# Spectral block: three real products per complex column, rows on row halves, later statistics in the MLP

## Chip, core and metric

One core of a Trainium2 chip runs the whole program. The metric is device microseconds, the median of three runs.

## What is computed

The reference is a two-branch block on x of 2048 x 512 in float32, with six modulation vectors (sa, ca, ga, sb, cb, gb) from a small product of c and w_mod:

```python
h = _layernorm(x) * (1 + ca) + sa
x = x + ga * irfft2(rfft2(h) * (w_r + 1j * w_i))     # over both axes, 2048 x 512
h = _layernorm(x) * (1 + cb) + sb
x = x + gb * (mish(h @ w1 + b1) @ w2)                # 512 -> 1376 -> 512
```

## The kernel before

The Fourier transforms are matrix products, in three stages, and the MLP follows as the fourth.

- Stage one (16 tiles of 128 rows): forward row and column products.
- Stage two (8 pairs of lane groups, with their complex weights): p2_in, p2_mul, p2_prod, p2_out. p2_out (line 531) leaves in PSUM what store_d copies to d, the input of stage three; d is held as two big tiles of eight row tiles each. In p2_out 16 matmuls contract over 64 partitions each, the two row halves in turn. store_d (lines 393 and 394) copies real and imaginary parts, and stores the real part once more with the sign turned as a third part, so that one slice of 128 columns serves as [re, im] and the next as [im, -re]. z_out and p2_out of the last pair end the stage; apply_gate (line 581) is one more product.
- Stage three (16 tiles): p3_col does a tile's inverse column products, eight matmuls of 128 x 128 for four column groups j, with kc (real and imaginary constants, 1 MB each) as moving operand; ScalarE copies the result to e; p3_row does four row products with kiv on tile n - 1, and VectorE adds the result to x. Beside them runs `prep`, a table by step that prepares the MLP: load_w1 and split_w1 (12 pieces of w1; each is cast to a high part on ScalarE, and GpSimd subtracts it for the low part), load_w2, sum_w2 (four differences on GpSimd into the one tile tsum), split_w2 (high and low part of a group of w2, group t = 1 to 5), norm_sums (statistics of a row tile, lines 127 and 128), norm_scale (Ln and Exp on ScalarE, lines 131 and 132, then five small operations on VectorE), keep (two normalised tiles), transpose_in and split_in (their transposes, high and low part h2).
- The MLP: 8 blocks of 256 rows, six items each (item i = 0 is the short one, 96 of the 1376 columns). mlp(s) is one item: up(s), the first products (line 805); front(s), Mish on ScalarE (813); halves(s - 1), casts on ScalarE (765) and subtractions on VectorE (766); back(s), sums on VectorE (827); down(s - 2), the second products of the item two back (855; 846 for the short item). At i = 3 norm_pair normalises the next block's two tiles (161), at i = 4 they are transposed (693) and split (701, 705, 706). At i = 1 and 2 of the next block the results are gathered and added to x.

Everything is in manual order: each engine's queue is the order in which the code issues. All DMAs go through SP's queue. Buffers come from rings of two: y, t, g1, g2, h in SBUF, and the PSUM banks A to D (two of each). The two loads of a w2 group take the two y buffers, so a group's load waits until the sums and splits of the group before are done.

Of the kernel before, what the change touches and what calls it, by code (L numbers as in the profile page):

```python
# [12 lines left out]
P = 128  # L13
# [18 lines left out]
def tile_spectral_block(ctx: ExitStack, tc: tile.TileContext, x_d, w1_d, b1_d, w2_d,  # L32
# [117 lines left out]
    def norm_scale(lo, hi):  # L150
        w = hi - lo
        pair = bank("C" if hi < N2 else "D")
        r, done = pair[:, 0:w], pair[:, 4:4 + w]
        norm_guess(lo, hi, r)
        norm_refine(lo, hi, 1, r, done)
        nc.vector.scalar_tensor_tensor(nmr[:, lo:hi], mv[:, lo:hi, 0], -1.0, done, op0=ALU.mult, op1=ALU.mult)
# [229 lines left out]
    dd = [big.tile([P, 8, 4, 3, NQ], F32, name=f"d{i}", tag=t) for i, t in enumerate(("da", "db"))]  # L386

    def store_d(ps, q0, nq, i, eng=None):
        src = ps[:, (4 - nq) * P:].rearrange("p (q a c) -> p a c q", q=nq, c=2)
        dst = dd[i].rearrange("p n d c q -> p (n d) c q")  # L390
        s = src[:, 32 * i:32 * i + 32]
        if eng is None:
            nc.scalar.copy(dst[:, :, 0:2, q0:q0 + nq], s)
            nc.scalar.mul(dst[:, :, 2, q0:q0 + nq], s[:, :, 0, :], -1.0)
# [177 lines left out]
    def mod_gate():  # L572
# [11 lines left out]
    kc = []  # L584
    wqb = pw.tile([P, 4, 2, 512], F32, name="wqb", tag="half")
    with tc.manual_schedule():
# [13 lines left out]
        for p in range(pairs):  # L600
# [50 lines left out]
    w2hi = pm.tile([P, 7, 256], F32R, name="w2hi")  # L651
# [56 lines left out]
    def p3_col(n):  # L708
        d = dd[n // 8][:, n % 8]
# [8 lines left out]
        st["e", n] = e  # L718

    def p3_row(n):  # L720
        e = st.pop(("e", n))
        px = bank("B")
        for j in range(4):
            nc.tensor.matmul(px[:, j * P:(j + 1) * P], e[:, j * P:(j + 1) * P], kiv[:, j, :],  # L724
                             start=True, stop=True)
        xn = x[:, n, :].rearrange("p (a b) -> p a b", b=4)
        nc.vector.tensor_tensor(xn, xn, px.rearrange("p (b a) -> p a b", b=4), op=ALU.add)

    def w2_space(t):
        if t == 2:  # L730
# [3 lines left out]
            w2[3] = [w2hi, v[:, 2]]  # L734
            w2["lo"] = w[:, 5376:5888]
        if t == 4:
# [4 lines left out]
            w2[0] = [w[:, 5376:5888], w2["lo"]]  # L741

# [21 lines left out]
    def split(h, l, r):  # L764
        nc.scalar.copy(h, r)  # L765
        nc.vector.tensor_tensor(l, r, plain(h), op=ALU.subtract)  # L766

    def split_w2(t, sums):
# [5 lines left out]
        if t == 3 and sums:  # L774
            nc.scalar.copy(h[:, 768:], tsum.rearrange("p e d -> p (e d)"))
        elif sums:
            split(h[:, 768:], l[:, 768:], tsum.rearrange("p e d -> p (e d)"))
# [382 lines left out]
```

## Time and profile before

| | us |
|---|---|
| median of three runs | 377.82 (377.52 to 378.47) |
| the profiled execution | 376.28 |
| its span, first to last instruction | 374.3 |
| stage three on PE, first column to last row | 90.6 to 135.7 |
| busy: PE, VectorE (DVE), ScalarE (ACT), GpSimd (POOL) | 368.0, 261.6, 213.9, 91.3 |

The granted TensorE clock was 0.998 throughout. PE is the matmul row, PEld its weight loads. A line of the chain or of a timeline has the start in us from the span's first instruction, the length, engine and line; in brackets stands how long the engine had been idle, and who released it. A profile counts each fp32 matmul as two records.

### The profile page before, as it was taken

The numbers are of one execution on the slowest core, as the hardware profiler recorded it, in microseconds if no ns is written. First come the engines' busy times: TensorE is split into PE (matmuls) and PEld (weight loads), VectorE is DVE, ScalarE is ACT, GpSimd is POOL, SyncE is SP. The second block draws the span as 40 slices with busy tenths as digits, with TensorE's granted clock in tenths as the row PEclk, the third lists the DMA queues.
The fourth block names the chain that finished last, engine by engine and source line by source line (L and its number), as shares of the span: only waits on it lengthen the run. The fifth ranks groups of instructions, "written<-read, shape, count | busy, mean of one in ns | idle before, by whom it ended". The sixth has DMA issues, their size and how long they took to land.

```text
span 374.3 us, 8202 instructions
## 1 busy us (share of the span) xinstructions
PE 368.0 (98%) x3245; PEld 349.6 (93%) x3245; DVE 261.6 (70%) x585; ACT 213.9 (57%) x487; POOL 91.3 (24%) x110
## 2 busy tenths in 40 slices
PE   8999999999999999999999999999999999999995
PEld 7899866658999999999999999999999999999995
DVE  2898989893878978767537646655754764776982
ACT  1788856855668447754634634654564563574540
POOL 0687725871884302300000000000000010017000
PEclk9999999999999999999999999999999999999999
DMA  7999998453332311000100100100100200212011
GB/s 253 380 321 350 341 383 310 146 199 132 105 89 70 101 30 57 2 2 0 59 2 0 58 3 0 58 2 0 58 1 2 80 0 2 81 56 90 2 56 56
DMA packets 20164, 36.81 MB, mean 98 GB/s; under 512 B 3712, under 2 KB 6624, under 8 KB 19872
## 3 DMA queue, kind: packets, MB, share of 16 engines
q1 hardware_dynamic: 20128, 36.31, 28.1%
q8 instruction: 25, 0.41, 0.4%
q14 instruction: 11, 0.09, 0.1%
HBM read 32.10 MB, written 4.20 MB: 97 GB/s over the span
## 4 chain that ended last, share of the span: by engine, by line
PE 94%; DVE 2%; DMA 1%; ACT 1%; issue 1%; SPq 0%; ACTq 0%
PE bank L805 32%; PE bank L855 24%; PE bank L531 4%; PE bank L504 4%; PE bank L715 4%; PE bank L714 4%; PE bank L724 4%; PE bank L211 3%; PE bank L256 3%; PE bank L846 3%; PE bank L871 2%; PE bank L693 2%; PE bank L479 1%; DMA wmc<-in_w_mod_dram 1%; PE bank L257 1%; PE bank L258 1%
## 5 line engine op out<-in xcount | busy, mean ns | idle before, releaser
L766 DVE TENSOR_TENSOR al<-buf,ah 128x512 fp32r<-128x512 f32 (+2 forms) x85 | 51.8, 629 | 63.1 <-ACT ah L765 62.9
L813 ACT ACTIVATE buf<-bank,b1n 128x256 f32<-128x256 f32 (+1 forms) x88 | 37.3, 471 | 90.8 <-PE bank L805 76.7
L805 PE MATMUL bank<-h2e,w1h 128*128 128x256 f32 (+1 forms) x352 | 62.3, 279 | 0.0
L805 PE MATMUL bank<-h2o,w1h 128*128 128x256 f32 (+1 forms) x352 | 62.1, 278 | 0.0
L805 PEld LDWEIGHTS bank<-h2e,w1h 128*128 128x128 f32 (+1 forms) x352 | 52.8, 185 | 0.0
L805 PEld LDWEIGHTS bank<-h2o,w1h 128*128 128x128 f32 (+1 forms) x352 | 52.8, 185 | 0.0
L805 PE MATMUL bank<-h2e,w1l 128*128 128x256 f32 (+1 forms) x176 | 48.8, 277 | 0.0
L805 PE MATMUL bank<-h2o,w1l 128*128 128x256 f32 (+1 forms) x176 | 48.8, 277 | 0.0
L785 POOL TENSOR_TENSOR buf<-buf,modr 128x512 f32<-128x512 f32 (+1 forms) x3 | 3.9, 1297 | 179.6 <-DMA buf<-in_B_w_dram 150.8
L765 ACT CAST ah<-buf 128x512 fp32r<-128x512 f32 (+2 forms) x85 | 43.3, 554 | 2.6 <-PE bank L871 1.6
L827 DVE TENSOR_TENSOR buf<-buf 128x128 f32<-128x128 f32 x148 | 42.5, 328 | 1.3
L855 PE MATMUL bank<-w2a,ah 128*128 128x256 f32 x161 | 33.3, 278 | 0.0
L805 PEld LDWEIGHTS bank<-h2e,w1l 128*128 128x128 f32 (+1 forms) x176 | 32.6, 185 | 0.0
L805 PEld LDWEIGHTS bank<-h2o,w1l 128*128 128x128 f32 (+1 forms) x176 | 32.6, 185 | 0.0
L855 PE MATMUL bank<-w2b,ah 128*128 128x256 f32 x147 | 30.6, 277 | 0.0
L855 PEld LDWEIGHTS bank<-w2a,ah 128*128 128x128 f32 x161 | 26.1, 188 | 0.0
L715 PE MATMUL bank<-kc,d 128*128 128x128 f32 x128 | 24.8, 275 | 0.0
L714 PE MATMUL bank<-kc,d 128*128 128x128 f32 x128 | 24.7, 275 | 0.0
L855 PEld LDWEIGHTS bank<-w2b,ah 128*128 128x128 f32 x147 | 24.0, 188 | 0.0
L127 DVE BATCH_NORM_STATS2 st<-x 128x6 f32<-128x512 f32 x32 | 22.1, 689 | 0.6
L701 ACT ACTIVATE buf<-bank,cols 128x256 f32<-128x256 f32 x32 | 16.3, 560 | 8.9 <-PE bank L693 8.9
L256 PE MATMUL bank<-buf,mring 128*128 128x512 f32 x48 | 20.7, 430 | 0.3 <-DVE buf L249 0.2
(228 smaller groups left out, 913.5 us busy)
## 6 DMA issues: line engine op xcount, KB each, us to landing
buf<-in_B_w_dram SPq DMA_DIRECT2D x20, 256.0 KB, 2.7
x<-in_A_x_dram SPq DMA_DIRECT2D x16, 256.0 KB, 4.9
xring<-in_x_t_dram SPq DMA_DIRECT2D x16, 256.0 KB, 4.9
out_dram<-x SPq DMA_DIRECT2D x7, 512.0 KB, 3.8
mraw<-in_km_dram SPq DMA_DIRECT2D x16, 128.0 KB, 4.7
wqa<-in_w_q_dram SPq DMA_DIRECT2D x4, 512.0 KB, 6.3
early<-in_w_mod_dram SPq DMA_DIRECT2D x8, 256.0 KB, 6.5
wqb<-in_w_q_dram SPq DMA_DIRECT2D x4, 512.0 KB, 7.2
```

Of the source, the lines that this page charges most:

```text
L127: nc.vector.bn_stats(t, x[:, n, :])
L256: nc.tensor.matmul(pa, m[:, a, 0:128], g, start=(i == 0), stop=False)
L504: nc.tensor.matmul(pb[lanes * h:lanes * h + lanes], kf[:, lanes * c:lanes * c + lanes], z_of(p, h), start=True, stop=True)
L701: nc.scalar.activation(t[:, 256 * e:256 * e + 256], ps[:, 256 * e:256 * e + 256], AF.Identity, bias=cols[:, 1, 0, k:k + 1], scale=cols[:, ...
L714: nc.tensor.matmul(o, dj[:, 0:128], kc[0][:, n, :], start=True, stop=False)
L715: nc.tensor.matmul(o, dj[:, 64:192], kc[1][:, n, :], start=False, stop=True)
L765: nc.scalar.copy(h, r)
L766: nc.vector.tensor_tensor(l, r, plain(h), op=ALU.subtract)
L805: nc.tensor.matmul(o, (w1h, w1l)[p][:, k, fs], h[:, k, q], start=(e == 0 and k == 0 and i == 0), stop=(e == len(tiles(t)) - 1 and k == 3 a ...
L813: nc.scalar.activation(w[:rows, 256 * e:256 * e + 256], o, AF.Mish, bias=b1n[:rows, f:f + 1])
L827: nc.vector.tensor_tensor(o, p, q, op=op)
L855: nc.tensor.matmul(o, a[p][:, e], w2[t][q][:, r], start=(own and half == 0 and t == 1 and i == 0), stop=(end and i == 2 and (n, half) != ( ...
```

## The change

1. store_d stores real and imaginary parts only. A new d_sum on GpSimd adds them per tile, as the third part (128 x 256). For tiles 0 and 1 it works in two pieces, the second one behind the last store.
2. p3_col: with a the real and b the imaginary part, and constants k0, k1, k2 (kc now holds re, -re - im, im - re, in four quarters by tile, 768 KB each), one product is (a + b) k0, and the results are (a + b) k0 + b k1 and (a + b) k0 + a k2. Each is two matmuls of 128 x 128 (line 729). ScalarE copies the first, 128 x 256, to SBUF (731); VectorE adds it to both others, 128 x 512, into a ring of three tiles e (733).
3. p3_row works on two tiles: 16 matmuls over 64 partitions, row halves in turn (746), and two adds to x on VectorE (749). It is issued behind the column products of the tile after the two.
4. norm_sums runs for tiles 0 to 3 in stage three; for tiles 4 to 15 in the MLP, one at i = 5 and one at i = 0, and norm_scale then at i = 3 of six blocks. So ScalarE needs Ln and Exp between two Mish.
5. prep is rewritten: w1's pieces in another order and through g1 and g2; the splits of w2's groups 2 and 3 on GpSimd; group 3's split in the MLP's items 2 and 3 (table `tail`), group 4's in 4, group 5's in 5 and 6. The first products of items 1 and 0 are issued around the last p3_row.
6. mod_gate, the constants and banks follow suit.

```diff
 def norm_scale(lo, hi):
-        pair = bank("C" if hi < N2 else "D")
+        pair = bank("D")
...
 def store_d(ps, q0, nq, i, eng=None):
-            nc.scalar.copy(dst[:, :, 0:2, q0:q0 + nq], s)
-            nc.scalar.mul(dst[:, :, 2, q0:q0 + nq], s[:, :, 0, :], -1.0)
...
+        (nc.scalar.copy if eng is None else eng.tensor_copy)(dst[:, :, 0:2, q0:q0 + nq], s)
+    def d_sum(n, late=None):
+        d = dd[n // 8][:, :, n % 8].rearrange("p c d (g j) -> p c d g j", j=8)
+        gs = slice(None) if late is None else slice(0, 8, 7) if late else slice(1, 7)
+        nc.gpsimd.tensor_tensor(d[:, 2, :, gs], d[:, 0, :, gs], d[:, 1, :, gs], op=ALU.add)
...
 def p3_col(n):
-        pe = bank("A")
-        for j in range(4):
-            dj = d[:, j].rearrange("p c q -> p (c q)")
-            o = pe[:, j * P:(j + 1) * P]
-            nc.tensor.matmul(o, dj[:, 0:128], kc[0][:, n, :], start=True, stop=False)
-            nc.tensor.matmul(o, dj[:, 64:192], kc[1][:, n, :], start=False, stop=True)
-        e = buf("g1")
-        nc.scalar.copy(e, pe)
+        d = dd[n // 8][:, :, n % 8].rearrange("p c d q -> p c (d q)")
+        k = kc[n // 4][:, n % 4]
+        if n % 2 == 0:
+            st["k1"] = bank("B")
+        both, one = bank("A"), st["k1"][:, 256 * (n % 2):256 * (n % 2) + 256]
+        k1 = buf("t")[:, 0:256]
+        for o, part, c in ((one, 2, 0), (both[:, 0:256], 1, 1), (both[:, 256:], 0, 2)):
+            for h in range(2):
+                nc.tensor.matmul(o[:, h * P:h * P + P], d[:, part, h * P:h * P + P], k[:, c, :], start=True, stop=True)
+            if c == 0:
+                nc.scalar.copy(k1, one)
+        st["e", n] = e = ering[:, n % 3]
+        nc.vector.tensor_tensor(e.rearrange("p (c s) -> p c s", c=2), both.rearrange("p (c s) -> p c s", c=2),
+                                k1.unsqueeze(1).to_broadcast([P, 2, 256]), op=ALU.add)
...
+    def p3_row(m):
+        px = bank("C"), bank("C")
+        for i in range(2):
+            e = st.pop(("e", 2 * m + i))
+            for h in range(2):
+                o = slice((2 * i + h) * P, (2 * i + h + 1) * P)
+                for c in range(2):
+                    j = 2 * c + h
+                    for r in range(2):
+                        rs = slice(64 * r, 64 * r + 64)
+                        nc.tensor.matmul(px[r][:, o], e[rs, j * P:j * P + P], kiv[rs, j, :], start=(c == 0), stop=(c == 1))
...
 def split_w2(t, sums):
+        eng = nc.gpsimd if t in (2, 3) else nc.vector
...
 def mlp(s, parts):
         if i == 3 and nxt:
+            if nxt > 2:
+                norm_scale(nxt, nxt + 2)
             norm_pair(nxt)
...
+        if i == 5 and b < NB - 2:
+            norm_sums(2 * b + 4)
+        if i == 0 and 0 < b < NB - 1:
+            norm_sums(2 * b + 3)
...
+    order = [0, 2, 3, 5, 6, 8, 9, 11, 1, 4, 7, 10]
+    def w1_next(i):
+        split_w1(order[i])
+        if i + 2 < len(order) and i not in (6, 7):
+            load_w1(order[i + 2])
...
+        2: ((w1_next, 2), (split_w2, 1, False)),
+        4: ((w1_next, 3), (norm_scale, 0, 2)),
+        5: ((sum_w2, 1, 2, 3), (keep, 0), (load_kc,)),
+        10: ((split_w2, 1, True), (norm_scale, 2, 4), (w1_next, 8), (load_w2, 0, None, slice(None), "h")),
...
-    for s in range(N2 + 1):
-        if s < N2:
-            p3_col(s)
-        if s >= 1:
-            p3_row(s - 1)
+    for s in range(N2):
+        if s + 2 < N2:
+            d_sum(s + 2)
+        p3_col(s)
+        if s % 2 == 0 and s:
+            p3_row(s // 2 - 1)
...
+    tail = {
+        2: ((sum_w2, 3, 0, 1, 2, 3), (split_w2, 3, False)),
+        3: ((split_w2, 3, True), (load_w2, 4)),
+        4: ((sum_w2, 4, 0, 1, 2, 3), (split_w2, 4, False), (split_w2, 4, True), (load_w2, 5)),
+        5: ((sum_w2, 5, 0, 1, 2, 3), (split_w2, 5, False)),
+        6: ((split_w2, 5, True),),
+    }
```

PE in the middle of stage three. Before, a tile's four row products stand behind the next tile's eight column products; L693 are block 0's transposes:

```order
L714 MATMUL bank<-kc_1104,d_756 128x128
L715 MATMUL bank<-kc_1240,d_756 128x128
L714 MATMUL bank<-kc_1104,d_756 128x128
L715 MATMUL bank<-kc_1240,d_756 128x128
L724 MATMUL bank<-kiv,buf 128x128 x4
L693 MATMUL bank<-ident,buf 128x128 x4
```

After, on the same engine from the stage's first column on (L729 columns, six a tile; L746 a pair's rows):

```order
L729 MATMUL bank<-kc_1092,d_756 128x128 x18
L746 MATMUL bank<-kiv,ering 128x128 x16
L729 MATMUL bank<-kc_1092,d_756 128x128 x6
L729 MATMUL bank<-kc_1220,d_756 128x128 x6
L746 MATMUL bank<-kiv,ering 128x128 x16
L729 MATMUL bank<-kc_1220,d_756 128x128 x12
L746 MATMUL bank<-kiv,ering 128x128 x16
```

The rows of two tiles now stand behind the columns of a third.

VectorE in stage three, before: each L727 adds a tile's rows to x, and the statistics of that tile follow (with norm_scale's five small operations in places):

```order
L727 TENSOR_TENSOR x<-x,bank 128x512
L127 BN_STATS st<-x 128x6
L128 BN_AGGR mv<-st 128x2
L727 TENSOR_TENSOR x<-x,bank 128x512
L127 BN_STATS st<-x 128x6
L128 BN_AGGR mv<-st 128x2
L141 SCALAR_TENSOR_TENSOR ve<-mv,bank 128x2
```

After, the same engine at step 10 (L733 makes e, L789 is split_w2's 1024-column subtraction):

```order
L733 TENSOR_TENSOR ering<-bank,buf 128x512 x2
L749 TENSOR_TENSOR x<-x,bank 128x2x2x128 x2
L789 TENSOR_TENSOR w_1359<-modr,w_1358 128x1024
L141 SCALAR_TENSOR_TENSOR ve<-mv,bank 128x2
L141 SCALAR_TENSOR_TENSOR ve<-ve,bank 128x2
L141 SCALAR_TENSOR_TENSOR rstd<-ve,bank 128x2
L141 SCALAR_TENSOR_TENSOR bank<-ve,bank 128x2
L156 SCALAR_TENSOR_TENSOR nmr<-mv,bank 128x2
L733 TENSOR_TENSOR ering<-bank,buf 128x512 x2
```

The first L733 of the last row is tile 11's e; it now stands behind the adds, the subtraction and the small operations.

ScalarE at items 3 and 4 of an MLP block, before:

```order
L813 ACTIVATE buf<-bank,b1n 128x256 x2
L765 CAST ah<-buf 128x384
L765 CAST ah<-buf 128x512
L161 ACTIVATE buf<-x,nmr,rstd 128x512 x2
L813 ACTIVATE buf<-bank,b1n 128x256 x2
```

And after, in the blocks that prepare tiles 4 to 15:

```order
L835 ACTIVATE buf<-bank,b1n 128x256 x2
L788 CAST ah<-buf 128x384
L788 CAST ah<-buf 128x512
L131 ACT_TABLE_LOAD
L131 ACTIVATE bank<-mv,eps 128x2
L132 ACT_TABLE_LOAD
L132 ACTIVATE bank<-bank 128x2
L161 ACTIVATE buf<-x,nmr,rstd 128x512 x2
L835 ACT_TABLE_LOAD
L835 ACTIVATE buf<-bank,b1n 128x256 x2
```

Five instructions came in between the casts of item 3 and Mish of item 4; there is a table load ahead of Ln, of Exp and of Mish.

More of the change, by code (lines that the diff above doesn't have):

```diff
@@ L584, in tile_spectral_block, with load_kc @@
     kc = []
+    def load_kc():
+        i = len(kc)
+        kc.append(big.tile([P, 4, 3, P], F32, name=f"kc{i}", tag=("cr", "ci")[i % 2]))
+        nc.sync.dma_start(kc[i], kc_d[:, 4 * i:4 * i + 4])
     wqb = pw.tile([P, 4, 2, 512], F32, name="wqb", tag="half")
@@ L635, in tile_spectral_block @@
             if p in (3, 5):
-                i = p // 2 - 1
-                kc.append(big.tile([P, N2, P], F32, name=f"kc{i}", tag=("cr", "ci")[i]))
-                nc.sync.dma_start(kc[i], kc_d[:, i, :, :])
+                load_kc()
+        for n in range(2):
+            d_sum(n, False)
         z_out()
         p2_out(pairs - 1)
+        for n in range(2):
+            d_sum(n, True)
         apply_gate()
@@ L650, in tile_spectral_block @@
     w2[1] = [pm.tile([P, 7, 256], F32R, name=f"w2{i}") for i in range(2)]
-    w2hi = pm.tile([P, 7, 256], F32R, name="w2hi")
+    ering = pm.tile([P, 3, 512], F32, name="ering", tag="w2hi")
     shift(ctx, 7)
@@ L661, in load_w1 @@
         k, lo, hi = piece(i)
-        r = buf("t" if i in (2, 3) else "g2")[:, 0:hi - lo]
+        r = buf("g1" if i % 3 == 1 else "g2")[:, 0:hi - lo]
         nc.sync.dma_start(r, w1v[:, k, lo:hi])
@@ new lines, in p3_col @@
+        st["e", n] = e = ering[:, n % 3]
[9 more added lines that the diff above has]
+                    j = 2 * c + h
+                    for r in range(2):
+                        rs = slice(64 * r, 64 * r + 64)
+                        nc.tensor.matmul(px[r][:, o], e[rs, j * P:j * P + P], kiv[rs, j, :], start=(c == 0), stop=(c == 1))
+        xm = x[:, 2 * m:2 * m + 2, :].rearrange("p n (a h r) -> p r n h a", h=2, r=2)
+        for r in range(2):
+            nc.vector.tensor_tensor(xm[:, r], xm[:, r], px[r].rearrange("p (n h a) -> p n h a", n=2, h=2), op=ALU.add)
@@ L741, in w2_space @@
             w2[0] = [w[:, 5376:5888], w2["lo"]]
+            w2[3][0] = pm.tile([P, 7, 256], F32R, name="w2hi", tag="w2hi")
     def item(g):
@@ L748, in tiles, with load_w2 @@
         return [(0, NF - 1, F - (NF - 1) * P)] if t == 0 else [(e, 2 * t - 2 + e, P) for e in range(2)]
-    def load_w2(t, spare=None, part=slice(None)):
+    def load_w2(t, spare=None, part=slice(None), tag="y"):
         rs = st["w2", t] = st["w2", t] if part.start else []
         for e, f, rows in tiles(t)[part]:
-            r = buf("y")[:rows] if spare is None else spare[:, e]
+            r = buf(tag)[:rows] if spare is None else spare[:, e]
             nc.sync.dma_start(r, w2_d[f * P:f * P + rows, :])
@@ L762, in sum_w2, with split @@
             nc.gpsimd.tensor_tensor(tsum[:, o], a, b, op=ALU.subtract)
[L764 removed]
+    def split(h, l, r, eng=nc.vector):
         nc.scalar.copy(h, r)
[L766 removed]
+        eng.tensor_tensor(l, r, plain(h), op=ALU.subtract)
     def split_w2(t, sums):
@@ L773, in split_w2 @@
         h, l = (w.rearrange("p e d -> p (e d)") for w in (hi, lo))
[L774 to L777, printed above, removed]
+        eng = nc.gpsimd if t in (2, 3) else nc.vector
+        if sums:
+            split(h[:, 768:], l[:, 768:], tsum.rearrange("p e d -> p (e d)"), eng)
         else:
             u, v = st["w2", t]
-            split(h[:, 0:256], l[:, 0:256], u[:, 0:256])
-            split(h[:, 256:768], l[:, 256:768], v)
+            split(h[:, 0:256], l[:, 0:256], u[:, 0:256], eng)
+            split(h[:, 256:768], l[:, 256:768], v, eng)
     def gate_w2(t):
@@ L798, in up @@
         ups[g] = []
-        ps = bank("CD"[g] if g < 2 else "A")
+        ps = bank("BD"[g] if g < 2 else "A")
         for e, f, rows in tiles(t):
@@ L1044, in _constants @@
     ki = ki / (S * D)
+    ki = ki.reshape(2, 64, 2, 2, 128).transpose(3, 1, 0, 2, 4)
     def matrix(shape, fn):
```

93 lines of the change are left out of this document (32 added, 61 removed).

## Prediction

> **What bounds the kernel now.** I read the page's first and fourth parts, then the chain of waits in order of time, then the timelines of stage two's end, of stage three and of one MLP block.
>
> ```profile
> PE 368.0 (98%) x3245; PEld 349.6 (93%) x3245; DVE 261.6 (70%) x585; ACT 213.9 (57%) x487; POOL 91.3 (24%) x110
> ```
>
> TensorE is busy for 98% of the span. So a matmul taken out is time gained, unless another engine then makes PE wait; today hardly any does. The chain of waits (start, length, what) gives the prices:
>
> ```profile
> 70.53 1.84 PE bank L531 x32
> ...
> 74.61 1.99 PE bank L531 x32
> ...
> 86.61 0.49 issue
> 87.10 2.45 PE bank L531 x32
> 89.55 1.05 PE bank L581 x2
> 94.18 0.89 PE bank L724 x8
> 96.86 0.89 PE bank L724 x8
> ```
>
> The reader is to see the pitch of stage three: from one tile's row products (L724) to the next is 2.68 us for eight column and four row matmuls, without a gap. The four rows take 0.89, so a matmul is 0.223.
>
> **Gain 1, columns.** Six column matmuls instead of eight: 1.34 us a tile for 1.79. Over 16 tiles that is -7.1 us, if PE is never kept waiting.
>
> **Cost 1, rows.** Two tiles now take 16 matmuls of 64 rows, two row halves in turn. p2_out (L531) issues exactly that: 16 in 1.84 us at 70.53, where 64-row transposes precede it, and 1.99 at 74.61, where a 128-row stage (L504) does. I take 1.99, since 128-row columns precede it here. Eight times 1.99 is 15.9, against 16 x 0.89 = 14.2: +1.7 (with 1.84: +0.5).
>
> **Gain 2, the end of stage two.** The negated third part isn't stored any more; these are ScalarE's rows there:
>
> ```profile
> 86.42 0.40 ACT L393 COPY d<-bank 128x256 f32<-128x256 f32 x1
> 86.67 0.33 ACT L394 ACTIVATE d<-bank 128x128 f32<-128x128 f32 x1
> ...
> 87.09 0.36 ACT L394 ACTIVATE d<-bank 128x128 f32<-128x128 f32 x1
> ```
>
> PE's 0.49 of "issue" at 86.61 ends as the store at 86.67 does, and the second bank of that p2_out is free at 87.45; that is why it took 2.45 and not 1.99. Without the L394 rows both waits go: up to -0.95. The new sum d_sum of tile 0 on POOL comes between the last store and the first column, beside the 1.05 of L581; I take -0.8 (bounds 0 and -1.0).
>
> PE's side therefore gives -7.1 + 1.7 - 0.8 = **-6.2 us**. Now what other engines ask back.
>
> **Stage three: who is late next.** PE now asks for a tile each 2.33 us (two columns and a row pair are 4.67), and its row products wait for a sum on DVE (L733), which waits for a copy on ACT (L731), in queues that also carry the weight preparation.
>
> ```profile
> 107.75 1.27 POOL L670 TENSOR_TENSOR w1l<-buf,w1h 128x512 fp32r<-128x512 f32 x1 [0.87 <-ACT w1h L669]
> 106.15 0.73 POOL L762 TENSOR_TENSOR modr<-buf,modr 128x256 f32<-128x256 f32 x1
> 93.07 0.62 ACT L669 CAST w1h<-buf 128x512 fp32r<-128x512 f32 x1
> 107.38 0.12 DVE L141 SCALAR_TENSOR_TENSOR ve<-mv,bank 128x2 f32<-128x2 f32 x1
> 107.99 0.16 DVE L156 SCALAR_TENSOR_TENSOR nmr<-mv,bank 128x2 f32<-128x2 f32 x1
> L727 DVE TENSOR_TENSOR x<-x,bank x16: 655/684/689, 96.9 to 135.8; 128x512 f32<-128x512 f32 x16
> L766 DVE TENSOR_TENSOR w<-buf,w x2: 1243/1500/1758, 94.1 to 95.3; 128x256 fp32r<-128x256 f32 x1, 128x512 fp32r<-128x512 f32 x1
> L766 DVE TENSOR_TENSOR w2b<-buf,w2b x2: 418/550/683, 145.8 to 146.2; 128x256 fp32r<-128x256 f32 x1, 128x512 fp32r<-128x512 f32 x1
> buf<-in_B_w_dram SPq DMA_DIRECT2D x20, 256.0 KB, 2.7
> ...
> kc<-in_kc_dram SPq DMA_DIRECT2D x2, 1024.0 KB, 5.2
> ```
>
> The two L766 rows are the same pair of subtractions, of 256 and 512 columns: 0.42 and 0.68 alone, 1.24 and 1.76 at 94.1 while POOL ran its own. So a DVE operation with two SBUF inputs and POOL take turns; L727, with one input in PSUM, stays at 0.68. And POOL is now nearly full: 14 sums of 0.73 (10.2), twelve low parts of at most 1.27 (14 to 15), eight sums of w2 (5.8) and the split of group 2 (0.73 + 1.27 + 2.5): 35 us in a stage of some 38.
>
> Laid out in queue order, four sums come late:
>
> - Tile 3 (rows of tiles 2 and 3). From the first column: product 0.45, copy 0.4, cast 0.62, POOL 1.27, then w1's third piece may load (issue 0.4, landing 2.7), its cast, the first w2 cast (0.4): at 6.9 DVE starts the w2 pair, then its 0.69. In turns with POOL that ends at 6.9 + 3.0 + 0.69 = 10.6, alone near 8.7. PE asks after five columns and one row pair, 5 x 1.34 + 1.99 = 8.7. Late by 0 to 1.9; POOL's queue never empties there, so I take 1.2.
> - Tile 11. Behind the rows of tiles 8 and 9 DVE has two adds (1.37), a 1024-column subtraction (1.23, the DVE row further down), five small operations (0.77, the rows 107.38 to 107.99) and then the sum, 0.69: 4.05, against two columns, 2.68. Late by 1.35 (2 if POOL has its turn).
> - Tiles 5 and 9. Tile 5: 1.37 + 0.77 + 0.69 = 2.83 for 2.68, 0.15. Tile 9 follows a transpose: ACT 1.02 and 0.62, DVE 0.69 twice, 3.0 for 2.68: with hand-overs 0.4.
>
> Together **+3.1** (1.2 + 1.35 + 0.55; bounds 1.6 and 5). A quarter of kc (768 KB) lands within the 5.2 that 1024 KB took, and is asked for in step 5, two columns, a row pair and a transpose (5.1) ahead of tile 8: nothing, or 0.5 if it queues. d_sum runs two tiles ahead: nothing. The statistics that leave DVE here are what makes room for its sums; the 12 that go to the MLP fall into DVE's idle time, 0.87 twice in a block where DVE has 12 us free:
>
> ```profile
> 170.70:200.00 29.30, 29.30 (x259) 29.30 (x259) 17.39 (x42) 15.34 (x32) 0.00 (x0) 1.00 0.05 19
> ```
>
> (The third to fifth busy times are DVE's, ACT's and POOL's.)
>
> **Table loads in six MLP blocks.** norm_scale needs Ln and Exp, the MLP needs Mish. The order shows three loads a block: ahead of Ln, of Exp, and of the next Mish. Before, there was one, and the next ACTIVATE began 20 ns behind its end:
>
> ```profile
> 137.43 0.27 ACT L131 ACTIVATE bank<-mv,eps 128x4 f32<-128x4 f32 x1 [3.72 <-DVE mv L128]
> 137.73 0.16 ACT L132 ACTIVATE bank<-bank 128x4 f32<-128x4 f32 x1
> 137.90 1.28 ACT L813 ACT_TABLE_LOAD   x1
> 139.20 1.19 ACT L813 ACTIVATE buf<-bank,b1n 96x256 f32<-96x256 f32 x3
> ```
>
> [...]
>
> I follow ACT through the block at 175, with PE's times as they are:
>
> ```profile
> 176.00 1.03 ACT L765 CAST ah<-buf 128x384 fp32r<-128x384 f32 x2
> 176.93 1.52 ACT L161 ACTIVATE buf<-x,nmr,rstd 128x512 f32<-128x512 f32 x2
> 183.19 1.02 ACT L701 ACTIVATE buf<-bank,cols 128x256 f32<-128x256 f32 x2 [1.06 <-PE bank L693]
> 186.46 0.84 ACT L813 ACTIVATE buf<-bank,b1n 128x256 f32<-128x256 f32 x2
> 182.72 0.87 PE bank L693 x8
> 188.89 1.37 PE bank L805 x12
> 190.26 2.38 PE bank L855 x21
> ```
>
> Item 3's casts end at 177.03. Load, Ln (0.27), load, Exp (0.16): 180.0; DVE's five small ones: 180.9; the normalised pair (1.52): 182.4, and PE transposes it at 182.72. Mish load, Mish of item 4, its casts: 185.5. The four Identities and two casts (183.19 to 186.46, 3.25): 188.7, and DVE's last low half 0.69 later, 189.4; PE reads it half way through the 1.37 at 188.89, at 189.57. Mish of item 5 and the first cast of item 4: 190.0, read at 190.26. So the loads eat a slack of 2 to 3 us and leave 0.2 to 0.3 at three places. I take +0.3 for all six blocks, since one of them (the last) has another w2 cast in the queue (bounds 0 and +4).
>
> **The w2 chain at the MLP's start.** Group 3's split moves into items 2 and 3, and on POOL, so groups 4 and 5, which share two buffers and one tile of sums, move back:
>
> ```profile
> 151.11 0.73 POOL L762 TENSOR_TENSOR modr<-buf 128x256 f32<-128x256 f32 x1 [7.88 <-DVE w2b L766]
> 153.64 1.19 POOL L762 TENSOR_TENSOR modr<-buf,modr 128x256 f32<-128x256 f32 x1
> 163.36 1.23 DVE L766 TENSOR_TENSOR w2b<-modr,w2c 128x1024 fp32r<-128x1024 f32 x1 [0.27 <-ACT w2c L765]
> 166.04 2.38 PE bank L855 x21
> ```
>
> Before, group 5 is ready at 164.59 for products at 166.04. After, from the end of item 3's first products: Mish 0.84, casts 1.03, pair 1.52, cast of sums 1.05 (by columns as the 1.03), POOL's 1024 columns 2.5, four sums 3.7 (151.11 to 154.83), two subtractions 1.1, load 3.5, sums 3.7, cast 1.05, subtraction 1.23: 21.2. PE needs four second products (2.38), three first (2.74), 0.87, 1.37 and 1.0 of item 5's: 21.0. Late by 0.2 and what queues in between cost; I take **+1.0** (bounds 0 and 2.5).
>
> **Sum.** -6.2 + 3.1 + 0.3 + 1.0 = -1.8 us. The profiled execution took 376.28 (span 374.3, about 2.0 around it), the median of three runs is 377.82, 1.5 more; the span's change is carried over to the median: **376.0**.
>
> **Rivals.**
> - Less is asked back: POOL's turns cost little and the w2 chain is in time. Then only tiles 11 and 9 wait, 1.8: -6.2 + 1.8 = -4.4, 373.4. For it: in the stage before, POOL idled and yet DVE kept up. Against: POOL's 35 us.
> - All of it is asked back: stage three loses 5, the w2 chain 2.5: +1.6 at worst; half way there from my values, -0.2, 377.6, no change to measure. For it: the 1.24 and 1.76.
> - The table loads tip over (the side opposite to mine). The three slacks are 0.2 to 0.3; from there each further 0.1 on ACT in a block costs 0.6 in all. A block that is 0.9 late, as one more hand-over of 0.1 at each of ACT's dozen steps there would make it, costs 6 x 0.9 = 5.4 in place of my 0.3: -1.8 + 5.1 = +3.3, 381.1; half of that lateness, with the slack gone, 2.7: 378.4. I put it between them, 379.6, slower. Against: nothing else is new in ACT's queue there.
> [...]
>
> **Chances.** My forecast 0.45 (0.31 of it faster by over 0.3%, which is 1.1 us and about what can be told from no change); less asked back 0.16; all asked back 0.20 (0.15 no change, 0.05 slower); tipped over 0.15; a pause 0.04. Faster 0.47, same 0.29, slower 0.24. The range 373.0 to 379.6 leaves out the pause, the upper half of the tipping and the best of the second case; for my forecast alone it is 374.5 to 377.5.
>
> **What the profile after would show.** Right: L729 in runs of 18, 6 and 12 matmuls at 0.223, L746 pairs at 1.99, no "issue" ahead of the last L531, PE gaps ahead of the rows of tiles 2, 10 (1 to 1.5 each), three loads of 1.28 in each of six blocks with no gap on PE. Wrong: 64-row pairs above 2.1, a gap at every pair, d_sum named as what PE waits for (POOL the bound), or gaps ahead of L705 or of each block's first products (ACT the bound).

## The result: slower by 1.1%, and the profile after

The changed kernel takes 382.69 us (median of four runs, 380.78 to 383.0) against 378.11 of the kernel before, run beside it: a ratio of 1.0112, 95% interval 1.0075 to 1.0149. Run once more it took 382.82 against 377.08 (1.0135, 1.0103 to 1.0167). It was forecast at 376.0. The profiled execution was the fastest of the four, 380.78 us, with a span of 379.0. The ratios leave out the few runs of these experiments that fell into a slower state (up to 606.1 us); the medians include them.

The page after, first part:

```profile
PE 368.9 (97%) x3309; PEld 347.4 (92%) x3309; DVE 273.3 (72%) x608; ACT 230.9 (61%) x480; POOL 112.4 (30%) x134
```

PE should have been busy some 6 us less than its 368.0 before: 32 column products are gone, and the 64 more that the rows take, of half the rows each, were in the sum at 1.7. That PE is 0.9 us busier is the first hint: some products take longer than they did. The windows show where the time lies. Columns: from and to, length, then the busy times of PE, PEld, DVE, ACT and POOL, the granted clock, and the DMA engines' share and GB/s. Before, the first block (the others are as long) and the last stretch:

```profile
153.40:182.72 29.32, 29.32 (x259) 29.32 (x258) 20.72 (x45) 17.12 (x35) 1.43 (x2) 1.00 0.05 19
329.32:374.30 44.98, 41.22 (x353) 41.02 (x351) 32.23 (x56) 20.11 (x42) 8.37 (x6) 0.98 0.15 53
```

After, stage three (up to its last row), the way to the first block's transposes, three blocks, and the last stretch:

```profile
90.36:134.66 44.30, 43.39 (x481) 41.07 (x481) 32.58 (x53) 24.02 (x51) 35.72 (x39) 1.00 0.40 124
134.66:150.51 15.85, 15.85 (x141) 15.85 (x141) 11.12 (x22) 9.35 (x19) 7.90 (x8) 1.00 0.11 34
150.51:183.02 32.51, 30.51 (x259) 30.11 (x258) 26.68 (x55) 20.84 (x39) 5.85 (x8) 1.00 0.10 34
183.02:212.35 29.33, 29.33 (x259) 29.33 (x258) 19.49 (x50) 19.34 (x38) 0.00 (x0) 1.00 0.05 19
212.35:242.77 30.42, 30.42 (x260) 30.27 (x258) 19.56 (x50) 19.91 (x38) 0.00 (x0) 1.00 0.05 19
331.84:379.00 47.16, 41.76 (x354) 41.16 (x351) 34.05 (x57) 22.72 (x47) 7.38 (x6) 1.00 0.14 51
```

Each stretch runs from one block's transposes to the next. Set against the forecast (the last column, in its own terms):

| | before | after | difference | forecast |
|---|---|---|---|---|
| span's start to first column | 90.60 | 90.36 | -0.2 | -0.8 |
| first column to block 0's transposes | 62.80 | 60.15 | -2.65 | -2.3 |
| to the next block's transposes | 29.32 | 32.51 | +3.2 | +1.0 |
| five further blocks | 146.60 | 148.82 | +2.2 | +0.3, with the row below |
| last stretch | 44.98 | 47.16 | +2.2 | |
| span | 374.3 | 379.0 | +4.7 | -1.8 |

So the gain came, and the MLP gave back 7.6 us. What PE waited for in the changed kernel (in total, times, longest):

```profile
PE bank L877 <- DVE w2b L789: 1.7, 1, 1.7
...
PE bank L746 <- DVE ering L733: 0.9, 2, 0.7
PE bank L877 <- DVE modr L915: 0.9, 1, 0.9
PE bank L877 <- DVE modr L907: 0.6, 1, 0.6
PE bank L877 <- DVE al L789: 0.3, 1, 0.3
```

None of these lies in the blocks from 183.02 to 331.84, and yet the block at 212.35 is 1.1 us longer, with PE busy throughout; so is the one at 272.09 (30.43), while the two behind them are at 29.32. The chain of waits shows how (start, length, what); its first rows are of the end of stage two and of stage three:

```profile
83.99 1.99 PE bank L531 x32
...
109.00 1.34 PE bank L729 x12
...
123.45 2.88 PE bank L729 x24
126.33 1.99 PE bank L746 x32
...
213.23 2.83 PE bank L827 x24
...
218.53 1.42 PE bank L827 x12
219.95 2.68 PE bank L877 x21
222.63 2.83 PE bank L827 x24
```

Before, the same p2_out, and a block from up(0) on:

```profile
83.54 1.99 PE bank L531 x32
...
218.21 1.37 PE bank L805 x12
219.58 2.38 PE bank L855 x21
221.96 2.72 PE bank L805 x24
```

The same 24 products take 2.83 instead of 2.72, at the same granted clock of 1.00, and go on so to the end of the block. PE has two paces here: from the transposes on it has the slower one in both kernels (24 products in 2.83), and in the kernel before it returns to the faster one in the short item up(0).

### The profile page after: what moved, and what is told of

Its sections match the earlier page's. It is cut to its first block, busy times and chain, and to the rows that moved or that the text cites. A ratio compares the mean times of both kernels' runs of the same rounds, so it can differ in the third digit from the quotient of the medians.

```text
span 379.0 us, 8390 instructions
## 1 busy us (share of the span) xinstructions
PE 368.9 (97%) x3309; PEld 347.4 (92%) x3309; DVE 273.3 (72%) x608; ACT 230.9 (61%) x480; POOL 112.4 (30%) x134
## 4 chain that ended last, share of the span: by engine, by line
PE 87%; DVE 7%; ACT 2%; issue 2%; DMA 1%; SPq 0%; DVEq 0%; ACTq 0%
PE bank L827 31%; PE bank L877 22%; PE bank L531 4%; PE bank L504 4%; PE bank L729 4%; PE bank L746 3%; PE bank L211 3%; PE bank L256 3%; PE bank L868 3%; PE bank L893 2%; PE bank L705 2%; PE bank L267 1%; PE bank L479 1%; PE bank L257 1%; PE bank L258 1%
## 5 line engine op out<-in xcount | busy, mean ns | idle before, releaser
L789 DVE TENSOR_TENSOR al<-buf,ah 128x512 fp32r<-128x512 f32 (+2 forms) x85 | 52.0, 636 | 56.6 <-ACT ah L788 56.6
L827 PE MATMUL bank<-h2o,w1h 128*128 128x256 f32 (+1 forms) x352 | 63.4, 280 | 0.0
L849 DVE TENSOR_TENSOR buf<-buf 128x128 f32<-128x128 f32 x148 | 44.7, 343 | 1.3
L729 PE MATMUL bank<-kc,d 128*128 128x128 f32 x192 | 23.6, 279 | 0.0
L729 PEld LDWEIGHTS bank<-kc,d 128*128 128x128 f32 x192 | 22.1, 192 | 1.5 <-POOL d L397 0.8
L749 DVE TENSOR_TENSOR x<-x,bank 128x512 f32<-128x512 f32 x16 | 17.2, 1123 | 7.6 <-PE bank L746 7.6
L877 PE MATMUL bank<-w,ah 128*128 128x256 f32 x112 | 20.1, 280 | 1.5 <-DVE modr L915 0.9
```

The lines of the kernel that those rows point to most:

```text
L729: nc.tensor.matmul(o[:, h * P:h * P + P], d[:, part, h * P:h * P + P], k[:, c, :], start=True, stop=True)
L749: nc.vector.tensor_tensor(xm[:, r], xm[:, r], px[r].rearrange("p (n h a) -> p n h a", n=2, h=2), op=ALU.add)
L789: eng.tensor_tensor(l, r, plain(h), op=ALU.subtract)
L827: nc.tensor.matmul(o, (w1h, w1l)[p][:, k, fs], h[:, k, q], start=(e == 0 and k == 0 and i == 0), stop=(e == len(tiles(t)) - 1 and k == 3 a ...
L849: nc.vector.tensor_tensor(o, p, q, op=op)
L877: nc.tensor.matmul(o, a[p][:, e], w2[t][q][:, r], start=(own and half == 0 and t == 1 and i == 0), stop=(end and i == 2 and (n, half) != ( ...
```

## Experiments

Two theories stood at first. L: the table loads cost 4.4 us, 2.2 by that slower pace and 2.2 in the last stretch. Q and P: the w2 chain costs the 3.2 us of the first block. The rival S: it is the sums that VectorE took over.

### No table loads

```diff
 def norm_guess(lo, hi, r):
-        nc.scalar.activation(r, mv[:, lo:hi, 1], AF.Ln, bias=eps)
-        nc.scalar.activation(r, r, AF.Exp, scale=-0.5)
+        table = lo < 4
+        nc.scalar.activation(r, mv[:, lo:hi, 1], AF.Ln if table else AF.Identity, bias=eps)
+        nc.scalar.activation(r, r, AF.Exp if table else AF.Identity, scale=-0.5 if table else 0.5)
```

> The changed kernel with the two table functions of the first guess replaced by Identity for tiles 4 to 15: the same instructions, and no table load in the MLP (it leaves out the right scale of these tiles). Theory L, the loads cost 4.4 us: 2.2 in two blocks, where a hold of under 0.1 us in the short item of up(0) leaves PE at the slower of its two matmul pitches to the end of the block (30.42 instead of 29.32), and 2.2 at the end, where ScalarE is 2.3 us late, the low part of w2's first tile with it, and POOL's gating then collides with VectorE. L gives 378.3 us, every block from the second on at 29.3, the last stretch at 45.0 instead of 47.16, and no PE wait for L907 and L915. Rival S, the sums that VectorE has taken over in the blocks are the cause, not the loads: 382 to 383 us, with blocks of 30.4 and a last stretch of 47 still there.

Measured: 379.2 us, ratio 1.0045 (1.0025 to 1.0064). Its windows for the block that had been 30.42, and for the last stretch:

```profile
212.75:242.07 29.32, 29.32 (x259) 29.32 (x258) 19.54 (x50) 15.45 (x36) 0.00 (x0) 1.00 0.05 19
330.03:375.40 45.37, 41.46 (x353) 41.06 (x351) 32.30 (x57) 21.00 (x45) 7.35 (x6) 0.99 0.15 53
```

The slow blocks are gone, the last stretch is 1.8 shorter, and the waits for L907 and L915 are gone: 4.0 us in this trace, as L says. In the medians it is less: of the 4.6 and 5.7 us that the changed kernel lost in its two comparisons 1.8 are left, where L gave 0.2 (378.3 for 378.1). The profiled run was the fastest of seven.

### The statistics alone, in the kernel before

The edit is part 4 of the change, in the kernel before, with nothing else.

> The kernel before with one part of the change alone: sums and scale of tiles 4 to 15 moved from stage three into the MLP's blocks, with their table loads. Theory L: the end loses 2.2 us as in the changed kernel, and up to two blocks 1.1 each, less 0 to 0.3 in stage three: 380 to 382.5 us against 378.1. A rival by which the loads stay hidden: 377.8 to 378.5 us.

Measured: 382.52 us, 1.0142 (1.0119 to 1.0165), as much as the whole change lost. Three of its blocks look like this one, and they alternate with blocks of 29.32; its last stretch is 2.0 longer than before's:

```profile
185.47:215.90 30.43, 30.43 (x259) 30.27 (x258) 19.56 (x50) 19.91 (x38) 0.00 (x0) 1.00 0.05 18
```

### The loads alone, in the kernel before

```diff
         if i == 3 and nxt:
+            if nxt > 2:
+                norm_guess(nxt, nxt + 2, bank("D")[:, 0:2])
             norm_pair(nxt)
```

> The kernel before with nothing of the change but table loads: Ln and Exp of two numbers a row, into a bank that nobody reads, ahead of norm in the MLP's blocks (six blocks, 3 loads each); sums and scale of all tiles stay in stage three. Theory L, the loads alone make the loss of the kernel with the statistics moved (5.1 us: three blocks of 30.44 and a last stretch longer by 2.0): 380 to 382.5 us, since ScalarE is late by 2.6 to 3.9 us in these items. Rival S, the sums on VectorE and the wait for its small steps are needed for it: 377 to 378.5 us, blocks 29.32.

Measured: 377.59 us, 1.0019 (1.0004 to 1.0035). Theory L falls in this form: three loads in each of six blocks are hidden in the blocks. The median is 0.6 us longer; in the profile the last stretch is, by 1.15:

```profile
212.29:241.61 29.32, 29.32 (x259) 29.32 (x258) 17.36 (x41) 19.43 (x38) 0.00 (x0) 1.00 0.05 19
329.57:375.70 46.13, 41.48 (x353) 41.08 (x351) 33.60 (x57) 21.85 (x47) 8.44 (x6) 0.99 0.15 52
```

The second low half of the transposed tiles shows how near the edge that is. In this kernel, in the block at 212.29:

```profile
217.33 0.69 DVE L706 TENSOR_TENSOR h2o<-buf,h2o 128x512 fp32r<-128x512 f32 x1 [0.88 <-ACT h2o L705]
```

and in the changed kernel, in the block at 212.35, with the next low part:

```profile
218.37 0.69 DVE L718 TENSOR_TENSOR h2o<-buf,h2o 128x512 fp32r<-128x512 f32 x1 [0.88 <-ACT h2o L717]
219.51 1.21 DVE L789 TENSOR_TENSOR al<-buf,ah 128x384 fp32r<-128x384 f32 x2 [0.45 <-ACT ah L788]
```

The half is ready 5.73 us after the block's transposes began with the loads alone, and 6.71 in the changed kernel. PE reads it half way through up(0), in a product that starts at about 6.8.

### Loads and small steps, without the sums

The kernel before with norm_scale of tiles 4 to 15 in the MLP, the sums (norm_sums) left in stage three.

> The kernel before with the scale of tiles 4 to 15 (Ln, Exp, their table loads, and VectorE's five small steps between Exp and norm) in the MLP's blocks, and the sums of all tiles still in stage three. The loads alone cost 0.6 us, all of it at the end, and the statistics whole cost 5.1. By the traces the second low half is ready 1.3 us later than in the kernel before with the loads alone and 2.3 later with the small steps too, against a slack of about 1.6: Theory LS, loads and small steps one behind the other are what goes over the slack, and the sums on VectorE add nothing: two or three blocks of 30.4, a last stretch of 46.5 to 47.2, 379.5 to 382 us. Rival S, it takes the sums too: all blocks 29.32, 377.5 to 378.5 us.

Measured: 382.46 us, 1.0125 (1.0107 to 1.0143): Theory LS, with the same two signs: two blocks of 30.4, and a longer last stretch.

```profile
183.72:214.13 30.41, 30.41 (x259) 30.27 (x258) 18.08 (x46) 19.89 (x38) 0.00 (x0) 1.00 0.05 18
332.82:379.80 46.98, 41.78 (x353) 41.17 (x351) 33.94 (x57) 22.70 (x47) 8.48 (x6) 0.98 0.14 51
```

So the loads, and the wait of ScalarE for VectorE's five small steps behind Exp, are needed together: the loads alone left every block at 29.32, and so did the small steps without loads in the first experiment. No cost of the twelve sums shows (1.0125 without them in the MLP, 1.0142 with them). Rival S has fallen.

One load of the three looks avoidable, and no run here tried it. Line 305 of both kernels names a set of tables for Ln and Exp together (`preload_act_table_set("natural_log_exp_and_others")`), and the kernel before ran all its Ln and Exp behind that one load (1.28 us, at 0.74), the last of them at 137.43 and 137.73, with none between. In the blocks nothing names the set, and each pair has a load ahead of Ln and another ahead of Exp (1.28 each). With 1.28 us less, the low half that is ready at 6.71 would be ready at about 5.4, an estimate from these rows, earlier than the 5.73 that cost no block.

### Holding PE at up(0) on purpose

```diff
                 transpose_in(nxt, g)
+            for _ in range({1: 5, 3: 6, 5: 7}.get(b, 0)):
+                norm_sums(N2 - 1)
             for g in range(2):
```

> The kernel before with VectorE held back in three blocks alone: 5, 6 and 7 more sums of a tile (0.87 us each, of tile 15, whose results stay the same) ahead of the split of the transposed halves in the second, fourth and sixth block. VectorE had 3.5 us to spare there, so up(0) and the product behind it would be held for about 0.5, 1 and 2 us. Theory K, a hold at or behind up(0) leaves PE at the slower pitch to the end of the block (24 matmuls in 2.83 instead of 2.72): each of the three blocks is longer by its hold and 1.0 us more, 29.32 to about 30.8, 31.3 and 32.3, the undisturbed blocks between at 29.32; 381 to 383.5 us in sum. Rival, the pitch has nothing to do with holds: the blocks are longer by their holds alone, 29.8, 30.3 and 31.3.

Measured: 382.7 us, 1.014 (1.0116 to 1.0165). The blocks with 6 and 7 more sums:

```profile
241.64:272.31 30.67, 30.46 (x260) 30.23 (x258) 21.78 (x55) 15.44 (x32) 0.00 (x0) 1.00 0.05 18
301.64:334.20 32.56, 30.45 (x260) 30.22 (x258) 23.64 (x57) 15.44 (x32) 1.56 (x2) 1.00 0.08 25
```

Five more did not hold PE at all (29.32). With six, the block is 1.35 longer; with seven, 3.24. From the transposes to the product behind up(0) it is 8.04 and 9.94 us, against 7.55 in an undisturbed block, so PE is held for 0.49 and 2.39 in all. The other 0.86 and 0.85 are no hold: the chain behind the first one has the slower pace to the block's end (the first block's here).

```profile
249.68 2.47 PE bank L855 x21
...
267.00 2.83 PE bank L805 x24
```

Theory K is shown, at 0.85 us: that is what a hold at up(0) costs besides its own length, whether it is 0.49 or 2.39. The sizes I had expected of the holds were off, since VectorE had more to spare.

### The w2 chain: group 3's lows on VectorE

```diff
-        eng = nc.gpsimd if t in (2, 3) else nc.vector
+        eng = nc.gpsimd if t == 2 else nc.vector
```

> The changed kernel with the low parts of w2's third group on VectorE again instead of POOL. Theory Q, what is late at the MLP's start is the place of group 4's raw split, in ScalarE's queue behind the first block's transposes, since its buffers are what group 5's load waits for: nothing to gain, load 5 still at about 155 and the wait in down(5) still 1.3 to 2.0 us, the time within 0.8 us of the changed kernel's (382.7). Theory P, POOL is too slow for group 3's lows (4.7 us of subtractions): the wait of 1.7 goes, the next block keeps the fast pitch, 379.8 to 381.0 us.

Measured: 383.36 us, 1.0156 (1.0134 to 1.0178): nothing gained, the wait for w2b still 1.7 us. Theory P has fallen. The block is even longer than in the changed kernel (34.06 for 32.51), for another reason:

```profile
166.49:169.64 3.15, 3.15 (x14) 3.15 (x15) 1.18 (x5) 0.99 (x2) 0.00 (x0) 0.51 0.00 0
```

Behind the wait the granted clock was 0.51 for 3.15 us: half a clock, which costs 1.5 us (0.49 of 3.15).

### The w2 chain: one item earlier

```diff
+        eng = nc.gpsimd if t == 2 else nc.vector
...
-        3: ((split_w2, 3, True), (load_w2, 4)),
-        4: ((sum_w2, 4, 0, 1, 2, 3), (split_w2, 4, False), (split_w2, 4, True), (load_w2, 5)),
-        5: ((sum_w2, 5, 0, 1, 2, 3), (split_w2, 5, False)),
-        6: ((split_w2, 5, True),),
+        3: ((split_w2, 3, True), (load_w2, 4), (sum_w2, 4, 0, 1, 2, 3), (split_w2, 4, False), (load_w2, 5)),
+        4: ((split_w2, 4, True), (sum_w2, 5, 0, 1, 2, 3)),
+        5: ((split_w2, 5, False), (split_w2, 5, True)),
```

> The changed kernel with group 3's lows on VectorE and, besides, sums and raw split of w2's group 4, the load of group 5 and both splits of group 5 one item earlier in the queues. Theories P and Q both: group 5 ready ahead of down(5), the stretch from the first block's transposes to the second's 29.4 to 30.2 us instead of 32.51, the time 379.8 to 380.8 us. Against both, if the stretch stays at 32 or more: PE waits there for the sums or for the order of VectorE's work whatever the w2 chain does, 382.5 us.

Measured: 380.72 us, 1.0092 (1.0073 to 1.0111). The wait for w2b is gone; one of 0.5 for al is left, and the slower pace behind it, so the block is 30.76:

```profile
151.41:182.17 30.76, 30.23 (x260) 30.03 (x258) 25.52 (x54) 19.82 (x37) 5.73 (x7) 1.00 0.11 35
```

So Theory Q stands: what made group 5 late was the place of its chain in the queues, and not POOL's pace. The edit moves group 4's raw split (whose buffers the load waits for), the sums and the later splits together, so which of these places counts isn't separated. The gain of the block doesn't all reach the time of this profile: its last stretch is 48.90, since behind the waits for L907 and L915 the clock was at half again: 0.51 for 3.2 us from 353.24 on, where 15 products took 3.47 (21 take 2.47).

### The changed kernel once more

> The changed kernel as it is, once more, on the same chip as the next two. In the two kernels with an edit of the w2 chain PE ran at a granted clock of 0.51 for 3.2 us behind a hold of 2 us (150.6 + 15.9 us and 353.24 us), which cost 1.5 us each time; the first profile of the changed kernel had such holds at both places and no such stretch, and its run was the fastest of its kernel (380.78 against a median of 382.69). Theory H, the typical run of the changed kernel has one or two such stretches: median 382 to 383 us, and a profiled run of that length shows one at the first blocks or in the last stretch. Rival N, the runs differ at their start only (wmc's transfer), as the kernel before does: a run of that length shows no such stretch, and its first product is late by as much.

Measured: 382.82 us, 1.0135 (1.0103 to 1.0167). The profiled run, 383.75, has such a stretch behind the w2 wait, where the first profile had none:

```profile
167.59:171.00 3.41, 3.41 (x18) 3.41 (x19) 1.55 (x6) 1.17 (x2) 0.00 (x0) 0.58 0.00 0
```

Its block 0 is 1.5 longer for it (34.05). But two other runs with a mean granted clock of 1.00 took 382.79 and 382.86 us, so Theory H explains this run and not the median. Rival N fails too: the first product was no later, and the first column of stage three by 0.57 only. Stage three and the way to the first transposes took 0.75 more, with three waits for e and not two. What else moves a run by 2 us stays open; the kernel before scatters likewise (375.72 to 379.64 here).

### The stride of the adds

```diff
-        xm = x[:, 2 * m:2 * m + 2, :].rearrange("p n (a h r) -> p r n h a", h=2, r=2)
+        xm = x[:, 2 * m:2 * m + 2, :].rearrange("p n (a h r) -> p r n a h", h=2, r=2)
...
-        ... px[r].rearrange("p (n h a) -> p n h a", n=2, h=2) ...
+        ... px[r].rearrange("p (n h a) -> p n a h", n=2, h=2) ...
```

> The changed kernel with x read and written by the adds behind the row products at a stride of 2 elements instead of 4 (column a, then h, within a half), the PSUM side at 128. Theory X, it is x's stride that makes such an add 1.12 us instead of the 0.68 of before's, and VectorE's 0.44 more for each of 16 makes e late at row pairs 1, 2 and 5: an add at 0.68 to 0.9 us, waits for e of 0 to 1.0 us in sum instead of 0.9 to 1.8, the time 381 to 382.3 us. Rival: the adds stay at 1.12, since they read two tiles at once from PSUM, and the time stays within 0.5 us of the changed kernel's.

The groups of the changed kernel in stage three (count, busy us, mean ns), and then of this one:

```profile
L749 DVE TENSOR_TENSOR x<-x,bank 128x512 f32<-128x512 f32 x16 | 17.2, 1123 | 7.6 <-PE bank L746 7.6
```

```profile
L749 DVE TENSOR_TENSOR x<-x,bank 128x512 f32<-128x512 f32 x16 | 10.3, 684 | 8.4 <-PE bank L746 8.4
```

The first half of Theory X is shown: 1123 ns against 684 by the order of the elements alone. x's stride goes from 4 to 2, and PSUM's from 1 to 128; the kernel before, with 1 and 128, took 684 too, so it is x's. The waits for e went from three (1.5 us, on the same chip) to one of 1.0. The time, 381.15 us, 1.0103 (1.0074 to 1.0132), is lower than the changed kernel's on that chip, but the intervals overlap: inconclusive.

### All repairs together

The two edits above (early w2 chain, stride), the sums of tiles 4 and 5 in stage three again, and this guess in place of Ln and Exp in the MLP:

```diff
+    def norm_plain(lo, hi):
+        ...
+        nc.vector.tensor_scalar(v, mv[:, lo:hi, 1], EPS, None, op0=ALU.add)
+        nc.vector.tensor_scalar(r.bitcast(i32), v.bitcast(i32), 1, None, op0=ALU.arith_shift_right)
+        nc.vector.tensor_scalar(r.bitcast(i32), r.bitcast(i32), -1.0, float(0x5f3759df), op0=ALU.mult, op1=ALU.add)
+        for out in (r, r, rstd[:, lo:hi]):
+            ...
+            for o, a, one, op in ((t, v, 1.0, ALU.mult), (t, t, -0.5, ALU.mult), (out, t, 1.5, ALU.add)):
+                nc.vector.scalar_tensor_tensor(o, a, one, r, op0=op, op1=ALU.mult)
```

> The changed kernel with four edits at once: the first guess of the MLP's rstd on VectorE (a shift and a subtraction of the bits, two Newton steps) instead of ScalarE's Ln and Exp, so no table load in the MLP; w2's groups 3 to 5 as in the kernel with the early chain; the sums of tiles 4 and 5 in stage three again; x's stride of 2 in the adds. The first product of the columns and rows stays as changed. If theories L, Q and X are what the change lost by: 3.5 us less from the loads, 2 to 3 from the w2 chain, 0.5 to 1.5 from the adds, 374.5 to 377 us, below the kernel before. If the new rows and columns themselves cost what the whole change lost, 380 us or more.

Measured: 384.64 us, 1.0184 (1.0146 to 1.0221), a miss, with the highest median of all. I had not costed the small steps. First and last of the thirteen (L162 to L169) in the block whose transposes come at 211.13:

```profile
207.70 0.16 DVE L162 TENSOR_SCALAR va<-mv 128x2 f32<-128x2 f32 x1
...
210.07 0.16 DVE L169 SCALAR_TENSOR_TENSOR nmr<-mv,rstd 128x2 f32<-128x2 f32 x1
```

Each waits for the one before, one per 0.2 us: 2.5 us, and norm and the transposes behind them were late in every block (30.6 to 31.7 us from the second on). (The loop runs three Newton steps; the text above says two.)

### The small steps half a block earlier

```diff
         if i == 0 and 0 < b < NB - 1:
             if b > 1:
                 norm_sums(2 * b + 3)
+            norm_plain(2 * b + 2, 2 * b + 4)
```

The call ahead of norm goes.

> The combined kernel with one edit: the thirteen small steps of the guess on VectorE (2.55 us, one behind the other) stand a half block earlier, behind the sums in the item of up(0), where VectorE idled 3.2 us, instead of right ahead of norm. In the combined kernel they made norm late and PE waited 0.4 to 1.5 us ahead of each block's transposes, and 0.38 between them. Expected: these waits gone, all blocks 29.3 us, the last stretch about 45, the span about 372 and the time 373 to 375.5 us, below the kernel before (377). If theories L and Q were not what the change lost by, 380 us or more.

Measured: 373.98 us against 376.95 of before, 0.992 (0.9906 to 0.9934). Once more, for its profile:

> The combined kernel with the early small steps, once more for its profile. Its median was 373.98 us against 376.95 of before. Theories L and Q expect every block from the first transposes on at 29.3 to 29.4 us, PE without a wait of over 0.1 us from the end of stage three to the end, a last stretch of 45.0 to 45.5, and a span of 371.5 to 372.5 us; what is gained over the kernel before is then stage two's end and stage three with the MLP's start, 0.7 and about 3.2 us.

Measured: 374.79 against 377.84, 0.992 (0.9891 to 0.9949). This version beats both kernels. Its windows: stage three with the way to the first transposes, the first block, the last stretch:

```profile
91.95:151.56 59.61, 58.72 (x620) 56.48 (x621) 42.59 (x83) 33.84 (x72) 40.28 (x45) 1.00 0.32 102
151.56:182.17 30.61, 30.07 (x259) 29.87 (x258) 26.39 (x61) 17.96 (x36) 5.73 (x7) 1.00 0.11 35
328.77:374.10 45.33, 41.39 (x353) 41.06 (x351) 32.27 (x57) 20.10 (x42) 7.26 (x6) 0.99 0.15 53
```

All blocks but the first are 29.32 again, and the last stretch is within 0.35 of before's 44.98. Two waits were left, against what was expected: 0.9 for a tile's e (row pair 1) and 0.5 in the first block. Besides, in stage one PE waited 1.7 us for VectorE (L269 for L262), where the other profiles have 0.2 to 0.9 at the same place, and the first column was 1.35 later than in the kernel before. So the span was 374.1 and not 372, in a run that was the longest of four.

## Why the prediction was wrong, step by step

- **Gain 2, end of stage two: right.** From the last but one p2_out to the first column it is 7.06 us before (83.54 to 90.60) and 6.37 after (83.99 to 90.36), -0.7 for -0.8. Stage one had been 0.5 later, which is why the table shows -0.2.
- **Columns, rows and late sums: right in sum by luck, not in the terms.** -2.65 for -2.3. Six column products take 1.34 us and a row pair 1.99 as forecast, but behind the 64-row products of a row pair two tiles' columns take 2.88 and not 2.68 (at 123.45), and one tile's 1.53 and not 1.34 (at 128.31): 0.2 a pair, an estimated 1.4 in all, and the sum had nothing for it. The late sums were too high by more than that. The waits for e were 0.9 in the profile, where 3.1 had been added, and 1.5 in the second profile. Tile 3, costed at 1.2, waited in the second and not in the first; tile 11 at 1.35 waited 0.75. That the adds would take 1.12 and not 0.68 was missed and did not decide.
- **The w2 chain: mis-sized.** The step was "late by 0.2 and what queues in between", +1.0, bounds 0 and 2.5. It measured +3.2, and 4.7 with a half-clock stretch: holds of 2.0, and 1.2 behind them, most of it the slower pace, for which the sum had no term. The length of the chain was nearly right (its last cast ended at 163.07, forecast for 163.0 from the same start, 143.03); what queued in between was too low: sums of a tile (0.87) and a low part stood ahead of the last subtraction on VectorE, which began at 165.01.
- **Table loads: the step that failed.** The term was +0.3 for six blocks; it measured 2.2 in the blocks, and 2.2 more in the last stretch. ScalarE's order came out as laid out: the last low half was forecast for 6.68 us behind the block's transposes (189.4 for 182.72), and is ready at 6.71 in the slow blocks. In the block at 183.02, behind the one that the w2 chain held, it is ready at 6.42, and that block is fast. Here is that half in the fast block, with the seventh and eighth product of up(0), of which the eighth reads it; then these two products in the slow block, where the half is the row at 218.37 above, which ends at 219.06:

```profile
188.75 0.69 DVE L718 TENSOR_TENSOR h2e<-buf,h2e 128x512 fp32r<-128x512 f32 x1 [0.88 <-ACT h2e L717]
189.74 0.39 PE L827 MATMUL bank<-h2e,w1h 128*96 128x256 f32 x2
```

```profile
219.06 0.42 PE L827 MATMUL bank<-h2o,w1h 128*96 128x256 f32 x2
```

  Two things were wrong. The slack, given as 0.2 to 0.3, was counted to the start of the product that reads the half, with nothing for the way from VectorE to PE: in the slow block the half ends 0.11 ahead of the eighth product (in the fast one 0.41), and PE is held by 0.03 all the same. And the price per miss: I counted a hold at its own length, so "each further 0.1 costs 0.6 in all"; in fact holds of 0.03 in up(0) and 0.2 behind it (for al, the 2.68 in the chain above, for 2.47) cost 1.1, since PE keeps the slower pace from the first of them to the block's end, some 0.87 more, as in the kernel with the held blocks. Behind a slow block the half is ready 0.3 earlier again, so every second block is slow: +2.2 in five blocks. The sign that was to show the forecast right, "no gap on PE", came all the same: the slow block has PE busy for 30.42 of 30.42 us.
- **The last stretch: left out.** Only the +0.3 touched it ("another w2 cast in the queue"), and it cost 2.2. ScalarE is 2.3 us late there too, so w2's low part for the short item, the load behind it in SP's queue and POOL's gating move as well. POOL's gatings and VectorE's sums, before and after:

```profile
338.28 1.30 POOL L785 TENSOR_TENSOR raw<-raw,modr 128x512 f32<-128x512 f32 x1
341.81 3.09 DVE L827 TENSOR_TENSOR buf<-buf 128x128 f32<-128x128 f32 x4
```

```profile
343.17 5.92 POOL L807 TENSOR_TENSOR raw<-raw,modr 128x512 f32<-128x512 f32 x4
345.25 4.19 DVE L849 TENSOR_TENSOR buf<-buf 128x128 f32<-128x128 f32 x4
```

POOL's four gatings begin 11.3 us after the block's transposes instead of 9.0, and now lie fully beside VectorE's sums, right ahead of what PE waits for (L907, L915). Four such sums took 1.01 alone (at 335.86 before), and 3.09 and 4.19 in these rows; a gating took 1.30 at 338.28, and 1.48 as the mean of the four after. This order of events is read from the traces; no run moved the gatings alone. The loads alone cost 1.15 here, loads and small steps 2.0 (46.13 and 46.98 for 44.98).
- **Rivals.** "The table loads tip over" was the right one, at a chance of 0.15, and its 379.6 too low, as it, too, priced a hold at its length and had nothing for the last stretch. A pause behind a table load, given a chance of 0.04, shows behind none of the 18 loads in the changed kernel's blocks. One of them:

```profile
178.36 0.27 ACT L131 ACTIVATE bank<-mv,eps 128x2 f32<-128x2 f32 x1
178.64 1.28 ACT L132 ACT_TABLE_LOAD   x1
179.94 0.16 ACT L132 ACTIVATE bank<-bank 128x2 f32<-128x2 f32 x1
```

Exp begins 20 ns after its load ends.

## What to carry to other kernels

Where an engine runs without gaps, don't price a short hold at its length (here 0.49 of hold cost 1.35): look whether the same products have two lengths in the trace, and ask what brings the faster one back. The chain that "just fits" over six repeats missed here in two of them (30.42 and 30.43 for 29.32), so price the miss, not the slack. And when work is moved onto a busy engine, cost its latency in the queue (table load, hand-over, small dependent steps) one behind the other: the loads alone cost 0.2%, loads and steps together 1.25%.

## What the runs showed of the hardware

- **Two paces of PE at a granted clock of 1.00.** 24 products in 2.72 or 2.83 us, 21 in 2.38 or 2.47. In these traces it drops behind the transposes and behind the holds in the blocks (0.03 to 2.4 us), and comes back in the short item, whose weights are 96 columns wide, when that isn't held. Why is open; the records show no cause.
- **Half a clock for about 3.2 us behind some holds**, at a cost of 1.5 us: behind the wait of 1.6 to 1.7 us for w2b in two of the five profiles that have it (0.51 over 3.15 us, 0.58 over a stretch of 3.41), and behind the waits of 0.7 and 0.9 for L907 and L915 in one of those that have them (the early w2 chain, 0.51), but not behind one of 2.1 us in the kernel with the held blocks (1.00). What decides it, no run shows.
- **The stride of an fp32 operand in SBUF.** An add to x took 684 ns for 512 columns at a stride of 1 (the kernel before) or 2 elements (the order of the adds changed), 1123 at 4 (the changed kernel). No run had another stride, and none shows why.
